# Folding a column Fourier transform a second time, in a fused attention and Fourier-mixing kernel

## Chip, cores and metric

The kernel runs on one core of one Trainium2 chip. The time is the device time of one execution in microseconds. A core has five engines that run their own instruction streams and wait for one another through semaphores: TensorE (PE, matmuls; PEld is its weight load), VectorE (DVE), ScalarE (ACT), GpSimd (POOL) and SyncE (SP, which here only starts DMAs).

## What is computed

Cosine attention over 8 batches, 12 heads, 448 tokens and 64 dimensions, then on its output (448 x 768 per batch) a two-dimensional Fourier transform of which the real part is kept, a residual, a layer norm and a two-layer feed-forward network. Cut to the core:

```python
q_n = q / (norm(q) + 1e-6); k_n = k / (norm(k) + 1e-6)
attn = softmax(q_n @ k_n.T / tau)
x = (attn @ v)                       # as (batch, 448, 768)
X = np.fft.fft(x, axis=1)            # over the sequence
X = np.fft.fft(X, axis=2)            # over the columns
u = x + np.real(X)
un = (u - mean(u)) / sqrt(var(u) + 1e-6)
out = u + np.maximum(un @ w_ch1, 0.0) @ w_ch2      # 768 -> 3072 -> 768
```

## The kernel before

The program first collects all its operations in a list (`P.add`: engine, function, estimated duration, priority, what is read and written), lays out an order for each engine with a small scheduler, and then emits the instructions in that order with the waits that the data need. An operation that two engines can do (`("act", "dve")`) goes to the one that the scheduler finds free first. Lower priority numbers are more urgent: batch b has 10 + 100 b and a little more, the evacuations of the feed-forward part have -1, its matmuls 5000 + b. So the attention of a batch goes ahead of the feed-forward matmuls of older batches, which fill the rest of TensorE's time.

The transform is done with real matrices. Rows and columns are folded first: with cosines only the sum of a row and its mirror image counts, with sines only their difference. `fold` is called for the column blocks dj = 0, 1, 2 of 128 columns, as soon as the two head pairs that it needs are done (`X[j]`, `X[j + 3]`). It takes sums and differences over the rows (AC), then of column c and c + 384 (F, one part for even and one for odd output columns), and multiplies each block with the sequence's cosines and sines:

```python
            if j >= 3:
                self.fold(b, j - 3, pj)
    ...
    def fold(self, b, dj, pj):
        ...
        for i, o in ((0, AluOp.add), (2, AluOp.subtract)):
            P.add("dve", ... v.tensor_tensor(AC[:, i:i + 2], X[:, 0:2], X[:, 2:4], o), ...)
        for eo, o in ((0, AluOp.add), (1, AluOp.subtract)):
            P.add("dve", ... v.tensor_tensor(F[:, eo, :, 128 * dj:128 * dj + 128],
                                             AC[:, :, 0, :], AC[:, :, 1, :], o), ...)
        def fn(pe):                                        # L828: 8 matmuls a block
            for eo in range(2):
                for s in range(2):
                    o = self.PS[:, bk + eo, s * NK:(s + 1) * NK]          # NK = 225
                    for t in range(2):
                        n = 128 if t == 0 else RB                         # RB = 97
                        r = pe.matmul(o, F[0:n, eo, 2 * s + t, dj * 128:dj * 128 + 128],
                                      self.CSs[0:n, t, s, :], start=(t == 0), stop=(t == 1))
        ...                                                # L839 (ACT) or L840 (DVE): PSUM to Tt
```

The column transform then takes all three blocks, for two tiles (kt) of sequence frequencies:

```python
        for kt in range(2):
            def fn(pe, tile=tile, kt=kt):                  # L863: 12 matmuls a tile
                for dj in range(3):
                    for s in (1, 0):
                        for eo in range(2):
                            m0, m1 = (0, 193) if eo == 0 else (193, 385)
                            o0 = (3 * eo + dj) * SQ2 + s * NK + 128 * kt
                            r = pe.matmul(PS[:, bk + s, m0:m1], self.Tt[:, o0:o0 + 128],
                                          self.CSd[:, dj, s, m0:m1], ...)
            ...           # L869, L872, L884: the two halves combined, x added, into U
```

The table CSd of cosines and sines for the columns (128 x 3 x 2 x 385) is made once, while batch 0's attention runs: its arguments by POOL and DVE (L403, L434, L439, L441, L442), the sines by ACT (L449, L450). After the transform comes the layer norm (L911 to L920; the normalised tile UN shares F's memory), then a transpose (for batch 0 by TensorE, later by DMA, L942), then the feed-forward part. Even batches have three tiles of 128 tokens, odd ones four, because one tile holds the last 64 tokens of two batches:

```python
        for ft in range(NF):                               # L974, L983/L984: relu(un @ w1)
            ...
        for i, ut in enumerate(tiles):                     # L995: hT @ w2
            for c in range(2):
                ...   # 24 matmuls of 384 columns, then on DVE (L1004) OUTB = PSUM + U
            if ut == A0:
                ...   # one plain store from SP
            else:
                ...   # one indirect store from POOL (L1019), rows in mirrored order
```

FFN b below means this part for batch b. While batch 0 is alone, idle time of TensorE is filled with matmuls whose result nobody reads (L1064).

The scheduler's rule for ACT and DVE, by which an engine that could start an operation at once may wait for a more urgent one instead (by at most 0.7 of the first one's duration):

```python
                    wait = tmin + 0.7 * op.durs[op.engs.index(e)]
                    t2, op2 = min((c for c in cands if c[0] <= wait), key=lambda c: (c[1].prio, c[0]))
                    if 109 <= op2.prio < 140 and op.prio > 200 or 9 <= op2.prio < 40 and (op.prio > 100 or op.prio > op2.prio + 0.5 and t2 < tmin + 0.25):
                        t, op = t2, op2
```

Of the kernel before, what the change touches and what calls it, by code (L numbers as in the profile page):

```python
# [12 lines left out]
DM = H * DH  # L13
# [8 lines left out]
ORDER = tuple(range(NJ))  # L22
# [39 lines left out]
class Plan:  # L62
# [54 lines left out]
    def schedule(self):  # L117
# [43 lines left out]
        while left:  # L161
            best = None
            for e in self.ENGS:
                cands = []
                for op in ready[e]:
                    rt = rtime(op, e)
                    if op.acquire is not None:
                        st = slot_time(op)
                        if st is None:
                            continue  # L170
                        rt = max(rt, st[0])
                    cands.append((max(rt, free[e]), op))
                if not cands:
                    continue
                tmin = min(c[0] for c in cands)
                t, op = min((c for c in cands if c[0] <= tmin + 1e-9), key=lambda c: (c[1].prio, c[1].seq))
                if e in ("act", "dve"):

                    wait = tmin + 0.7 * op.durs[op.engs.index(e)]
                    t2, op2 = min((c for c in cands if c[0] <= wait), key=lambda c: (c[1].prio, c[0]))  # L180
                    if 109 <= op2.prio < 140 and op.prio > 200 or 9 <= op2.prio < 40 and (op.prio > 100 or op.prio > op2.prio + 0.5 and t2 < tmin + 0.25):
                        t, op = t2, op2
                if best is None or (t, e) < best[:2]:
                    best = (t, e, op)
            t, e, op = best
            for e2 in op.engs:
                ready[e2].remove(op)
            op.eng = e
            if op.acquire is not None:
                for new, i in zip(op.acquire, slot_time(op)[1]):  # L190
                    old = slots[new.pool][i]
                    if old is not None:
                        op.deps.update(old.users)
                    slots[new.pool][i] = new
                    new.slot = i
            d = op.durs[op.engs.index(e)]
            op.start = t
            free[e] = t + d
            op.end = t + d
            if op.dma is not None:  # L200
                i = 1 if e == "pool" and op.name[:3] != "sc_" else 0
                t0 = max(op.end + DMA_LAT, dma_free[i])
                op.end = t0 + op.serve * (1.6 if dma_free[1 - i] > t0 else 1.0)
                dma_free[i] = op.end
            self.order[e].append(op)
            left -= 1
            for n in nxt.get(op, ()):
                cnt[n] -= 1
                if cnt[n] == 0:
                    put(n)  # L210
# [100 lines left out]
class Kern:  # L311

    def __init__(self, nc, q, k, v, w1, w2, out, tau, nb):
# [21 lines left out]
        self.X = T("X", [128, 4, DM])  # L335
        self.AC = T("AC", [128, 4, 2, 128])
        self.F = T("F", [128, 2, 4, DM // 2])
        self.Tt = T("Tt", [128, NJ * SQ2 + 32])
# [7 lines left out]
        self.CSd = T("CSd", [128, 3, 2, NL])  # L346
# [21 lines left out]
    def consts(self):  # L368
        P = self.P
        nd, ns = 3 * NL, 2 * NK  # L370
# [15 lines left out]
        def iotad(g):  # L386
            g.iota(self.rowf[:, 2:3], [[0, 1]], base=256, channel_multiplier=1, allow_small_or_imprecise_dtypes=True)
            g.iota(lcf[:, 0:193], [[2, 193]], base=0, channel_multiplier=0, allow_small_or_imprecise_dtypes=True)
            return g.iota(lcf[:, 193:385], [[2, 192]], base=1, channel_multiplier=0, allow_small_or_imprecise_dtypes=True)
# [7 lines left out]
        P.add("pool", iotad, 0.6, -7, "iotad", writes=["OUT1d", "rowg"])  # L397
# [24 lines left out]
        for p0, c0 in ((0, 64), (64, 129)):  # L422
# [3 lines left out]
                                 g.memset(self.Tt[:, NJ * SQ2:], 0.0))[-1],  # L426
# [4 lines left out]
        def args_d():  # L431
            P.add("pool", lambda g: prods(g, sd, lcf, 3, None, AluOp.mult), 3.75, 22, "tpd", reads=["OUT1d", "rowf", "rowg"],
                  writes=["tpd0", "tpd1", "tpd2"])
            P.add("pool", lambda g: g.tensor_scalar(Qt[:, sd], Pt[:, sd], 1.0 / DM, M, AluOp.mult, AluOp.add), 1.2, 23, "tqd",  # L434
                  reads=["tpd0", "tpd1", "tpd2"], writes=["tqd0", "tqd1", "tqd2"])
            for j in range(3):
                x, y = (a[:, NL * j:NL * j + NL] for a in (Pt, Qt))
                n = [f"tpd{j}", f"tqd{j}"]
                P.add("pool", lambda g, y=y: g.tensor_scalar(y, y, M, -float(DM), AluOp.subtract, AluOp.mult), 1.5, 25, "trd",  # L439
                      reads=n[1:], writes=n[1:])  # L440
                P.add("pool", lambda g, x=x, y=y: g.tensor_tensor(x, x, y, AluOp.add), 1.1, 25, "tad", reads=n, writes=n[:1])  # L441
                P.add("dve", lambda v, x=x, y=y: v.scalar_tensor_tensor(y, x, -1.0, x, AluOp.mult, AluOp.max), t_dve(NL), 30, "tmd",  # L442
                      reads=n, writes=n[1:])
        self.args_d = args_d

        def table(c, tab, n, k, sg, nm, pr, order, wr, t):
            def sins(a):
# [4 lines left out]
                         reads=[a + nm + x for a in ("tp", "tq") for x in ("012" if nm == "d" else [""])] + ["cst"], writes=[wr], order=order)  # L452
# [4 lines left out]
        self.table_d = lambda order: table(sd, self.CSd, DM, 3, -1, "d", 10, order, "CSd", 1.3)  # L457
# [227 lines left out]
    def attn(self, b):  # L685
# [34 lines left out]
        for pos, j in enumerate(ORDER):  # L720
# [78 lines left out]
            if j >= 3:  # L799
                self.fold(b, j - 3, pj)  # L800


    def fold(self, b, dj, pj):
# [3 lines left out]
        AC, F = self.AC, self.F  # L807
# [4 lines left out]
        for eo, o in ((0, AluOp.add), (1, AluOp.subtract)):  # L812
# [4 lines left out]
            if dj == 0 and eo == 0:  # L817
                self.first_f = op
        tile = Tile("G")

        def fn(pe):
            bk = self.bank(tile)
            for eo in range(2):
                for s in range(2):
                    o = self.PS[:, bk + eo, s * NK:(s + 1) * NK]
                    for t in range(2):
                        n = 128 if t == 0 else RB
                        r = pe.matmul(o, F[0:n, eo, 2 * s + t, dj * 128:dj * 128 + 128],  # L828
                                      self.CSs[0:n, t, s, :], start=(t == 0), stop=(t == 1))
            return r  # L830
        P.add("pe", fn, 8 * t_mm(NK), pj, f"fs{dj}_{b}", reads=[f"F0{dj}", f"F1{dj}", "CSs"], tiles=(tile,), acquire=tile, margin=0.2)

        for es, ah in ([(("act", "dve"), (0, 1))] if b == 0 and dj < 2 else [(("act",), (0,)), (("dve",), (1,))] if b == 0 else [(("act", "dve"), (0, 1))]):
            def ev(e, ah=ah):
                bk, a = self.bank(tile), slice(ah[0], ah[-1] + 1)
                o = self.Tt[:, 0:NJ * SQ2].rearrange("p (a d k) -> p d a k", a=2, d=3)[:, dj, a]
                i = self.PS[:, bk + ah[0]:bk + ah[-1] + 1, 0:SQ2]
                if e is self.nc.scalar:
                    return e.activation(o, i, ACTF.Copy)  # L839
                return e.tensor_copy(o, i)  # L840
            n = len(ah) * SQ2
            P.add(es, ev, [t_act(n) if e == "act" else t_dve(n) for e in es], pj, f"te{dj}_{b}",
                  writes=[f"Tt{dj}" + ("b" if len(ah) == 1 and ah[0] else "")], after=[tile.users[0]], tiles=(tile,))

    def fft(self, b):
# [6 lines left out]
        for kt in range(2):  # L852
            tile = Tile("G")

            def fn(pe, tile=tile, kt=kt):
                bk = self.bank(tile)

                for dj in range(3):
                    for s in (1, 0):
                        for eo in range(2):  # L860
                            m0, m1 = (0, 193) if eo == 0 else (193, 385)
                            o0 = (3 * eo + dj) * SQ2 + s * NK + 128 * kt
                            r = pe.matmul(PS[:, bk + s, m0:m1], self.Tt[:, o0:o0 + 128], self.CSd[:, dj, s, m0:m1],  # L863
                                          start=(dj == 0 and eo == 0), stop=(dj == 2 and eo == 1), skip_group_check=True)
                return r
            self.fd_ops.append(P.add("pe", fn, 12 * 0.081, pr + 1, f"fd{kt}_{b}", reads=["Tt0", "Tt1", "Tt2", "Tt2b", "CSd", "Tpad"],
# [36 lines left out]
        order = [A0, A1, Yt] if b % 2 == 0 else [A0, A1, Yt, Zt]  # L903
# [46 lines left out]


    def ffn(self, b):
# [3 lines left out]
        tiles = [A0, A1, Yt] if par == 0 else [A0, A1, Yt, Zt]  # L956
# [29 lines left out]
        for i, ut in enumerate(tiles):  # L986
            ob = self.out_next % 2
            self.out_next += 1
            for c in range(2):
                tile = Tile("M")  # L990
                for q4 in range(4):
                    def fn(pe, tile=tile, q4=q4, i=i, c=c):
                        bk = self.bank(tile)
                        for ft in range(6 * q4, 6 * q4 + 6):
                            r = pe.matmul(self.PS[:, bk, 0:384], self.hT[:, ft, 128 * i:128 * i + 128],  # L995
                                          self.W2b[:, ft, 384 * c:384 * c + 384], start=(ft == 0), stop=(ft == NF - 1))
                        return r
                    self.main = P.add("pe", fn, 6 * t_mm(384), PM, f"y{i}{c}{q4}_{b}",
# [3 lines left out]
                def fin(v, tile=tile, c=c, ut=ut, ob=ob):  # L1002
                    cs = slice(384 * c, 384 * c + 384)
                    return v.tensor_tensor(self.OUTB[:, ob, cs], self.PS[:, self.bank(tile), 0:384], self.U[:, ut, cs], AluOp.add)  # L1004
                rn = [f"U{ut}l", f"U{ut}h"] if ut != Zt else [f"U{ut}z{z}{x}" for z in (0, 64) for x in "lh"]
                P.add("dve", fin, t_dve(384), PEV, f"fin{i}{c}_{b}", reads=rn, writes=[f"OUT{ob}"] if c == 0 else [f"OUT{ob}b"],
                      after=(self.main,), tiles=(tile,))
            o = self.OUTB[:, ob, :]
# [114 lines left out]
```

## Time and profile before

| | |
|---|---|
| device time, median of 3 | 629.57 us (629.31 to 631.14) |
| span of the profiled execution | 629.2 us |
| busy: PE, DVE, ACT, POOL | 603.2, 382.8, 345.5, 97.7 us |
| sequence transform, L828 | 192 matmuls of 225 columns |
| column transform, L863 | 192 matmuls of 192 or 193 columns |
| feed-forward, L974 and L995 | 232.9 and 227.8 us busy |
| last matmul ends, span ends | 623.7, 629.2 us |

The page of a profile gives each engine's busy time, the same in 40 equal slices of the span, and the chain of work that ended last, followed back from the end; other views give the busy time in chosen stretches, the instructions in order of time, and who waited for whom. A line such as `L828 PE MATMUL PS<-CSs,F` names the line of the program, the engine, the operation, and what is written from what. Matmuls are pipelined, so the durations of single ones overlap.

### The profile page before, as it was taken

Reading aid. Unit: us, or ns where it says so; the run is one execution under the profiler, and the core shown is the slowest. Engines: PE = TensorE matmul, PEld = TensorE weight load, DVE = VectorE, ACT = ScalarE, POOL = GpSimd, SP = SyncE. Lnnn points to the kernel's source line nnn. Section 1 sums busy time; section 2 is a strip of 40 time slices with the busy share of each in tenths; the row PEclk is TensorE's granted clock in tenths of the full one; section 3 lists DMA queues with packets and bytes.
Section 4 is the critical chain, followed back from the end, with each engine's and each line's share of the span. In section 5 each row is a group of like instructions: output and inputs, shape, how many; then the busy total and the mean of one; then the engine's idle time right before and its main releaser. Section 6 shows DMA issues by size and latency. Waiting matters only on the chain.

```text
span 629.2 us, 13742 instructions
## 1 busy us (share of the span) xinstructions
PE 603.2 (96%) x5695; PEld 397.2 (63%) x5713; DVE 382.8 (61%) x869; ACT 345.5 (55%) x678; POOL 97.7 (16%) x129
## 2 busy tenths in 40 slices
PE   4798899999999999999999999999999999999996
PEld 4477677667876667665656765666566666654563
DVE  6978888896787876778777787747534550110011
ACT  7784797257862786376678638842864024114300
POOL 8822511110030102000300310003000010010001
PEclk8998999999999999999999999999999999999999
DMA  9999996977279517952973695139200130010011
GB/s 197 112 204 207 159 169 118 167 147 147 61 79 203 141 37 102 147 127 64 138 120 101 86 212 92 23 89 120 39 3 1 63 89 1 26 50 1 1 50 51
DMA packets 187486, 62.04 MB, mean 99 GB/s; under 512 B 166688, under 2 KB 185120, under 8 KB 187424
## 3 DMA queue, kind: packets, MB, share of 16 engines
q1 hardware_dynamic: 129504, 38.35, 32.9%
q0 software_dynamic: 57920, 22.81, 28.3%
q8 instruction: 45, 0.74, 0.5%
q14 instruction: 17, 0.14, 0.1%
HBM read 51.90 MB, written 11.01 MB: 100 GB/s over the span
## 4 chain that ended last, share of the span: by engine, by line
PE 91%; DVE 4%; ACT 3%; issue 1%; POOLq 0%; POOL 0%; ACTq 0%; DVEq 0%
PE PS L995 35%; PE PS L974 35%; PE PS L750 5%; PE PS L781 5%; PE PS L828 3%; PE PS L863 3%; PE PS L778 2%; ACT E L732 1%; PE PS L1064 1%; PE PS L610 1%; PE PS L762 1%; PE PS L763 1%; DVE UNT L574 1%; DVE UNT L570 0%; ACT E L544 0%
## 5 line engine op out<-in xcount | busy, mean ns | idle before, releaser
L974 PE MATMUL PS<-UNT,W1b 128*128 128x256 bf16 (+3 forms) x1422 | 232.9, 316 | 3.0 <-ACT hT L983 0.6
L995 PE MATMUL PS<-W2b,hT 128*128 128x384 bf16 x1344 | 227.8, 326 | 0.0
L974 PEld LDWEIGHTS PS<-UNT,W1b 128*128 128x128 bf16 x1440 | 129.9, 98 | 86.4 <-issue 4.9
L995 PEld LDWEIGHTS PS<-W2b,hT 128*128 128x128 bf16 x1344 | 129.4, 98 | 83.0 <-issue 1.8
L732 ACT ACTIVATE E<-PS 128x900 bf16<-128x900 f32 (+1 forms) x192 | 150.0, 826 | 29.3 <-PE PS L750 25.8
L983 ACT ACTIVATE hT<-PS 128x512 bf16<-128x512 f32 (+3 forms) x161 | 77.0, 478 | 100.7 <-PE PS L974 99.3
L1004 DVE TENSOR_TENSOR OUTB<-PS,U 128x384 f32<-128x384 f32 x56 | 31.1, 555 | 124.2 <-PE PS L995 123.7
L1019 POOL DMA_INDIRECT out_dram<-OUTB,IDX x20 | 21.3, 1064 | 307.7 <-DVE OUTB L1004 129.2
L984 DVE TENSOR_SCALAR hT<-PS 128x256 bf16<-128x256 f32 (+3 forms) x79 | 39.8, 505 | 25.8 <-PE PS L974 24.9
L667 DVE TENSOR_REDUCE SS<-QH 128x6 f32<-128x384 f32 x84 | 45.4, 541 | 11.2 <-ACT QH L665 11.0
L665 ACT ACTIVATE QH<-STG 128x384 f32<-128x384 f32 x84 | 43.6, 519 | 15.2 <-DVE SS L667 7.3
L781 PE MATMUL PS<-VB,E 128*128 128x65 bf16 x1152 | 51.3, 193 | 0.0
L712 POOL DMA_DIRECT2D VB<-in_v_dram x24 | 25.2, 1055 | 162.2 <-PE PS L781 161.6
L781 PEld LDWEIGHTS PS<-VB,E 128*128 128x128 bf16 x1152 | 47.8, 97 | 1.5
L750 PE MATMUL PS<-QT,KT 64*128 64x225 bf16 x576 | 43.0, 261 | 2.1 <-ACT E L732 1.6
L778 PE MATMUL PS<-VZ,E 128*128 128x130 bf16 x192 | 42.2, 220 | 0.0
L884 DVE TENSOR_TENSOR U<-SQT,X 128x384 bf16<-128x384 f32 (+3 forms) x80 | 41.0, 551 | 0.8
L674 DVE TENSOR_TENSOR QH<-STG,RN 128x768 bf16<-128x768 f32 x42 | 39.8, 952 | 1.3
L750 PEld LDWEIGHTS PS<-QT,KT 64*128 64x128 bf16 x576 | 21.2, 94 | 20.2 <-ACT E L732 7.2
L839 ACT ACTIVATE Tt<-PS 128x900 bf16<-128x900 f32 (+1 forms) x22 | 19.9, 904 | 25.6 <-PE PS L828 25.5
L795 DVE TENSOR_TENSOR X<-PS,RD 128x512 bf16<-128x512 f32 x48 | 33.1, 689 | 1.2
L793 DVE RECIPROCAL RD<-PS 128x8 f32<-128x8 f32 x48 | 9.8, 205 | 34.5 <-PE PS L781 34.4
(116 smaller groups left out, 498.8 us busy)
## 6 DMA issues: line engine op xcount, KB each, us to landing
STG<-in_q_dram SPq DMA_DIRECT2D x18, 384.0 KB, 6.0
STG<-in_k_dram SPq DMA_DIRECT2D x18, 384.0 KB, 4.6
VB<-in_v_dram POOLq DMA_DIRECT2D x24, 192.0 KB, 6.7
W1b<-in_moe_w_ch_dram POOLq DMA_DIRECT2D x12, 384.0 KB, 9.7
W2b<-in_moe_w_ch_dram POOLq DMA_DIRECT2D x12, 384.0 KB, 7.0
out_dram<-OUTB SPq DMA_DIRECT2D x8, 384.0 KB, 2.9
hT<-in_k_dram SPq DMA_DIRECT2D x2, 576.0 KB, 5.3
hT<-in_q_dram SPq DMA_DIRECT2D x2, 576.0 KB, 6.7
```

The source lines that it names most:

```text
L665: P.add("act", lambda a, sq=sq, src=buf[:, w * x:w * x + w]: a.activation(sq, src, ACTF.Square), t_act(w), pr, f"sq{i}_{b}", reads=bn, wri ...
L667: P.add("dve", lambda v, o=SS[:, i, H // ns * x:H // ns * (x + 1)], sq=sq: v.tensor_reduce(o, sq.rearrange("p (h d) -> p h d", d=DH), AX.X ...
L674: P.add("dve", lambda v, i=i, buf=buf, qh=qh: v.tensor_tensor(v3(qh), v3(buf), RN[:, i, :].unsqueeze(2).to_broadcast((128, H, DH)), AluOp. ...
L732: return a.activation(o, self.PS[:, bk:bk + nc_, 0:SQ2], ACTF.Exp, scale=1.0 / self.tau)
L750: i = pe.matmul(self.PS[:, bk + h, c0:c0 + NK], self.KT[r, jj, kt * 128:(kt + 1) * 128], self.QT[r, jj, cols], start=True, stop=True)
L778: pe.matmul(o, st(6), self.VZ[:, j, :], start=True, stop=False, skip_group_check=True)
L781: r = pe.matmul(o[:, 65 * h:65 * h + 65], st(2 * kt + h), self.VB[:, kt, 2 * j + h, :], start=False, stop=(h == 1 and kt == 2), skip_group ...
L884: return v.tensor_tensor(U[o0:o0 + n, ut, cs].rearrange("p (i e) -> p i e", e=2), src, X[i0:i0 + n, x, cs].rearrange("p (i e) -> p i e", e ...
L974: r = pe.matmul(self.PS[:, bk, 0:n], self.W1b[:, j, ft * 128:(ft + 1) * 128], unT[:, j, cs], start=(j == 0), stop=(j == NJ - 1))
L983: return e.activation(self.hT[:, ft, cs], self.PS[:, bk, 0:n], ACTF.Relu)
L984: return e.tensor_relu(self.hT[:, ft, cs], self.PS[:, bk, 0:n])
L995: r = pe.matmul(self.PS[:, bk, 0:384], self.hT[:, ft, 128 * i:128 * i + 128], self.W2b[:, ft, 384 * c:384 * c + 384], start=(ft == 0), sto ...
```

## The change

A second fold is put on top of the first. Column c of F and column 384 - c (with sum and difference, for cosine and sine) go into one column of a new array G of 193 columns, so that the transforms have a block of 128 and one of 65 columns in place of three of 128. Block 0 can be made after dj = 0 and dj = 2, block 1 after dj = 1, so the head pairs are taken in the order 0, 1, 2, 3, 5, 4. The two columns without a partner (0 and 192) are copied by POOL. The table CSd and its making shrink from three blocks to two; POOL clears all of Tt once. ACT and DVE may now wait for a more urgent operation of any older batch, not of batches 0 and 1 alone. And the last batch takes the tiles in another order, so that the very last store is a plain one from SP, done in two parts of 512 and 256 columns. The diff, cut:

```diff
-ORDER = tuple(range(NJ))
+NG = DM // 4 + 1
+ORDER = (0, 1, 2, 3, 5, 4)
@@ schedule
-                    if 109 <= op2.prio < 140 and op.prio > 200 or 9 <= op2.prio < 40 and (op.prio > 100 or op.prio > op2.prio + 0.5 and t2 < tmin + 0.25):
+                    if op2.prio >= 9 and (op.prio > op2.prio + 60 or op2.prio < 40 and op.prio > op2.prio + 0.5 and t2 < tmin + 0.25):
@@ buffers and tables
+        self.G = T("G", [128, 2, 4, NG])
-        self.Tt = T("Tt", [128, NJ * SQ2 + 32])
+        self.Tt = T("Tt", [128, 4 * SQ2 + 32])
-        self.CSd = T("CSd", [128, 3, 2, NL])
+        self.CSd = T("CSd", [128, 2, 2, NL])
-                                 g.memset(self.Tt[:, NJ * SQ2:], 0.0))[-1],
+                                 g.memset(self.Tt[:], 0.0))[-1],
-            for j in range(3):        # arguments of CSd, a block each
+            for j in range(2):
@@ fold
-            if j >= 3:
+            if pos >= 3:
                 self.fold(b, j - 3, pj)
+        if dj < 2:
+            c = 192 * dj
+            P.add("pool", lambda g: g.tensor_copy(G[:, :, :, c:c + 1], F[:, :, :, c:c + 1]), 0.25, pj, f"gc{dj}_{b}", ...)
+        if dj == 0:
+            return
+        blk = 2 - dj if dj == 2 else 1
+        c0, n, m = ((1, 127, 128), (128, 64, 65))[blk]
+        for i, o in ((0, AluOp.add), (1, AluOp.subtract)):
+            def fn(v, i=i, o=o):
+                ...
+                return v.tensor_tensor(gp(G[:], [[gs, 2], [NG, 2], [1, n]], g0 + c0), gp(F[:], [[fs_, 2], [384, 2], [1, n]], f0 + c0),
+                                       gp(F[:], [[fs_, 2], [384, 2], [-1, n]], f0 + 384 - c0), o)
+            P.add("dve", fn, t_dve(4 * n), pj, f"g{blk}_{b}", ...)
-                        r = pe.matmul(o, F[0:n, eo, 2 * s + t, dj * 128:dj * 128 + 128],
-                                      self.CSs[0:n, t, s, :], start=(t == 0), stop=(t == 1))
+                        r = pe.matmul(o, G[0:k, eo, 2 * s + t, blk * 128:blk * 128 + m],
+                                      self.CSs[0:k, t, s, :], start=(t == 0), stop=(t == 1))
@@ fft
-                for dj in range(3):
+                for d in range(2):
+                    k = 128 if d == 0 else NG - 128
...
-                            r = pe.matmul(PS[:, bk + s, m0:m1], self.Tt[:, o0:o0 + 128], self.CSd[:, dj, s, m0:m1],
+                            r = pe.matmul(PS[:, bk + s, m0:m1], self.Tt[0:k, o0:o0 + 128], self.CSd[0:k, d, s, m0:m1],
@@ feed-forward
+        return [A0, A1, Yt, Zt] if b < self.nb - 1 else [A1, Yt, Zt, A0]
...
+            very_last = b == self.nb - 1 and i == len(tiles) - 1
+            for c, (c0, c1) in enumerate(((0, 512), (512, 768)) if very_last else ((0, 384), (384, 768))):
...
+                if very_last:
+                    P.add("sp", ... sy.dma_start(<out, rows of the tile, columns c0:c0 + n>, self.OUTB[:, ob, c0:c0 + n]) ...)
```

## The prediction
> **What bounds the kernel now.** I read the page first (busy shares, then the slices), then the windows table of the whole span, then the chain that ended last, then the timelines of the stages in which the chain leaves TensorE.
>
> The page's first two parts:
>
> ```profile
> PE 603.2 (96%) x5695; PEld 397.2 (63%) x5713; DVE 382.8 (61%) x869; ACT 345.5 (55%) x678; POOL 97.7 (16%) x129
> ...
> PE   4798899999999999999999999999999999999996
> ...
> DVE  6978888896787876778777787747534550110011
> ...
> PEclk8998999999999999999999999999999999999999
> ```
>
> From the sixth slice on TensorE (PE) is never under nine tenths. The windows table, cut where the stages change (columns: stretch, its length, PE, weight loads, DVE, ACT, POOL busy, then clock and DMA):
>
> ```profile
> 0.00:56.40 56.40, 40.44 (x763) 33.02 (x764) 43.42 (x91) 40.98 (x60) 34.12 (x56) 0.92 1.13 181
> 56.40:134.20 77.80, 74.75 (x812) 55.16 (x810) 67.39 (x162) 49.69 (x114) 18.82 (x25) 0.99 1.07 154
> 134.20:485.30 351.10, 349.83 (x3322) 230.58 (x3338) 246.16 (x566) 226.26 (x448) 36.84 (x41) 1.00 0.65 99
> 485.30:623.70 138.40, 138.23 (x802) 78.45 (x802) 25.23 (x52) 28.60 (x57) 7.01 (x7) 1.00 0.10 35
> 623.70:629.20 5.50, 0.00 (x0) 0.00 (x0) 0.56 (x1) 0.00 (x0) 0.96 (x1) 0.90 0.18 72
> ```
>
> So there are four regimes. To 56.4 us a prologue, batch 0 alone, in which PE also runs filler matmuls and the path goes through DVE and ACT. To 134 us a stretch in which DVE is busy 67.4 of 77.8 us (87%) and PE 96%. From 134 to 623.7 us PE is idle for 1.27 + 0.17 = 1.4 us in all, so there a matmul taken away is time taken away. Last a tail of 5.5 us without PE. Because a busy PE need not be PE at its peak, I took the cost of the transform not from busy time but from the chain, which lists back-to-back steps (start, length, what). Batch 2:
>
> ```profile
> 178.07 0.79 PE PS L828 x8
> ...
> 181.01 0.79 PE PS L828 x8
> ...
> 189.58 0.79 PE PS L828 x8
> 190.37 1.95 PE PS L995 x12
> 192.32 2.02 PE PS L863 x24
> ```
>
> L828 is the sequence transform of one block (8 matmuls of 225 columns), L863 the column transform (24 matmuls of 192 or 193). Each sits directly in PE's chain, with the second feed-forward product (L995) around it.
>
> [...]the chain has 0.79/8 = 99 ns and 2.02/24 = 84 ns[...]. [...]the new 65-column weights should not be dearer than today's 128 columns (98 ns shown, hidden behind matmuls). No run here shows 65 yet. [...]
>
> **The change, part by part.**
>
> *Steady state, batches 2 to 7.* Sequence transform: three blocks become two, minus 1 x 0.79 us. Column transform: 24 matmuls become 2 tiles x 2 blocks x 2 x 2 = 16, minus 8 x 84 ns = 0.67 us. Together 1.46 us of PE time per batch, all on PE's path; six batches give 8.8 us. Added on DVE are four folding adds a batch, two of 508 and two of 256 elements. At the rate of the present pairs (two of 512 in 0.76 us) that is 0.76 + 0.5 = about 1.3 us a batch[...]. Taken from ACT: one eviction of 128x900, 0.92 us. Added on POOL: two copies of 8 elements, like the 6-element copies of L704 (212 to 805 ns). In this stretch DVE is 70% busy and ACT 64%, and the attention of a batch runs ahead of its feed-forward part (the last column transform is at 483 us, its feed-forward part starts at 561). So I count nothing for the additions.
>
> *Batch 1, 56 to 134 us.* Same PE saving, but FFN 1 has to have its input. The normalised second tile and the transposes on the way to it, and FFN 1's first matmul:
>
> ```profile
> 127.51 5.76 SPq L942 DMA_TRANSPOSE UNT<-F  x4
> 128.40 0.46 DVE L920 TENSOR_SCALAR F<-U,MV,RS 128x768 bf16<-128x768 bf16 x1
> 132.45 1.65 PE L974 MATMUL PS<-UNT,W1b 128*128 128x256 bf16 x12
> ```
>
> FFN 1 begins with two tiles. The second is normalised at 128.86 and its transpose lands a median 2.5 us after issue, about 131.5 us by my estimate. Spare time: 0.95 us. PE would arrive 1.46 us earlier, so at least 0.5 us of the saving becomes a wait; the DVE adds lengthen the wait and the eviction taken from ACT (91% busy from 80 to 100 us, 18.53 of 20) shortens it. I keep 0.7 of the 1.46 us.
>
> *Prologue, batch 0.* Its PE savings only make room for fillers. What counts is the other engines. Timeline of 26 to 33 us, and below it from the chain:
>
> ```profile
> 29.02 1.62 DVE L574 TENSOR_TENSOR UNT<-hT,RN 128x384 bf16<-128x384 f32 x1
> 29.20 1.02 POOL L441 TENSOR_TENSOR U<-U,UNT 128x385 f32<-128x385 f32 x1
> ...
> 31.24 0.54 DVE L442 SCALAR_TENSOR_TENSOR UNT<-U 128x385 f32<-128x385 f32 x1
> ```
>
> ```profile
> 39.65 0.93 ACT Tt L839
> ```
>
> The first lasts 1.62 us where its neighbours last 0.55: POOL's third table step runs beside it. With a table of two blocks the third POOL step is gone (minus 1.07 us on DVE), and so is the third L442 (minus 0.54). The eviction at 39.65 stands between exponentials on ACT and is gone for that position (minus 0.93). Back come the folding adds: the larger pair fits mostly into the gap of 1.1 us that DVE has before L840 at 42.5 us; the smaller pair is on the end of the chain (plus 0.5 to 0.75), and the first tile of the column transform ends 4 x 84 = 0.34 us sooner. Sum: -1.07 - 0.54 - 0.93 + 0.7 - 0.34 = -2.2 us. Now POOL also clears the whole of Tt at the start, 1,832 columns; by VZ's clearing (780 columns, 0.87 us) an estimate of 2 us, against 1.25 us saved in the first table step (3.74/3). I keep 1.7 of 2.2 us.
>
> *Tail.*
>
> ```profile
> 623.79 0.56 DVE L1004 TENSOR_TENSOR OUTB<-PS,U 128x384 f32<-128x384 f32 x1 [3.36 <-PE PS L995]
> ...
> 625.16 0.96 POOL L1019 DMA_INDIRECT out_dram<-OUTB,IDX  x1 [6.95 <-DVE OUTB L1004]
> ```
>
> Today a 384-column addition, then 0.8 us until POOL starts, then 3.1 us until an indirect store lands, then 0.9 us to the end. Afterwards: 256 columns ([...]0.43 us) and a plain store from SP. SP's full-tile stores land in 2.9 us; for a third of the bytes I estimate 2.4. 0.1 + 0.43 + 0.05 + 2.4 + 0.9 = 3.9 us against 5.5: minus 1.6 us. The products of the last tile cost PE the same in sum (24 x 512 + 24 x 256 columns, as 48 x 384).
>
> *The waiting rule and the order of heads.* They decide who goes first on DVE and ACT; for batches 0 and 1 the old rule did nearly the same already, and later PE does not wait for either. I count 0. Sum: -8.8 - 0.7 - 1.7 - 1.6 = -12.8 us, so 629.6 - 12.8 = 616.8 us.
>
> **The rivals.** (a) *DVE becomes the bound in 56 to 134 us.* For it: 87% busy, and only 0.95 us to spare before FFN 1. Against it: 10.4 us of DVE idle in that stretch. If all four adds of batches 0 and 1 (up to 4 us) delayed FFN 1, the gain of the prologue and of batch 1 would be gone: about 620 us. (b) *A wait for POOL takes the place of the matmuls.* The sequence transform now waits for a POOL copy, in a queue that holds loads of V (three of 1.05 us right after the last product of a batch) and stores. If each of 14 copies held PE for 0.3 us: 4 us, 620.5 us. Against it: these loads start some 3 us before the copy is due (246.72 to 249.86, the last fold done at 249.56), and the program's order was laid out with more than their real length. (c) *Only the count of matmuls moves*, the prologue being bound elsewhere: -8.8 - 0.7 - 1.6, 618.5 us. (d) *Everything lands*: batch 1 and the prologue in full, 1.3 us more: 615 us or a little under.
>
> **Range and chances.** 616.8 us as the middle; (a) and (b) in part give the upper end, 620.5, and (d) with a warmer prologue clock (0.92 on average now) the lower, 613.5. A 2% gain needs 617.0 us, which is almost my middle: 0.52 for faster, 0.47 for within 2%. Slower by 2% would need a stall of over 25 us, where PE has next to none: 0.01.
>
> **What would show each step right or wrong.** L828's successor with 128 matmuls, 0.79 us per block of 8, and the column transform with 128 in 1.35 us per batch; PE idle from FFN 1's start to the end of PE under 2 us; FFN 1's start about 3 us earlier with a short wait for the transposed input; the first feed-forward matmul near 54.7 us; a tail under 4 us. It is wrong if PE's list of waits names POOL copies or G, if FFN 1's first matmul waits for more than 2 us, if blocks of 65 weight columns take longer than 0.79 us, or if the first feed-forward matmul comes no earlier than 56.4 us.

## The result, and the profile after

The changed kernel takes 626.16 us (median of 4, 625.57 to 627.76), the kernel before beside it 630.36 us; the ratio is 0.9938, 95% interval 0.9911 to 0.9965. So it is faster by 0.6%, where 2.0% was predicted, and outside the predicted range.

The page's busy shares and slices of the changed kernel show at once where to look:

```profile
PE 594.1 (95%) x5607; PEld 388.3 (62%) x5625; DVE 391.3 (63%) x893; ACT 342.7 (55%) x677; POOL 98.4 (16%) x141
...
PE   4784889999999999999999999999999999999998
...
PEclk9996899999999999999999999999999999999999
```

PE has 9.1 us less busy time than before, but its fourth slice (47 to 63 us) has fallen to four tenths, and the clock that it was granted there to six. The windows table, with the same cuts as before:

```profile
0.00:56.40 56.40, 33.53 (x624) 27.20 (x625) 37.64 (x80) 35.73 (x52) 31.85 (x54) 0.90 1.13 182
56.40:134.20 77.80, 73.61 (x911) 57.14 (x910) 63.39 (x147) 48.13 (x104) 17.71 (x24) 0.96 0.91 122
134.20:485.30 351.10, 349.32 (x3278) 225.63 (x3291) 263.93 (x615) 229.85 (x464) 40.81 (x55) 1.00 0.66 105
```

In the prologue all four engines have less work done at 56.4 us than before; DVE 37.6 us in place of 43.4. None of them has become the bound; all of them wait. From 134 us PE is as full as before. PE's list of waits (what waited for what, us in all, times, longest) names the one long wait that is new:

```profile
PE PS L847 <- POOL G L823: 9.4, 1, 9.4
PE PS L1097 <- DVE ID L430: 5.6, 1, 5.6
PE PS L599 <- DVE QH L575: 1.8, 1, 1.8
```

L847 is the sequence transform, L823 the POOL copy of the columns without a partner. It is one single wait of 9.4 us. POOL's own timeline of 39 to 56 us tells why the copy came late:

```profile
39.90 0.82 POOL L470 DMA_DIRECT2D W1b<-in_moe_w_ch_dram  x1 [2.73 <-DMA W1b<-in_moe_w_ch_dram]
40.76 0.51 POOL L823 COPY G<-F 128x8 bf16<-128x8 bf16 x1
45.58 0.84 POOL L470 DMA_DIRECT2D W1b<-in_moe_w_ch_dram  x1 [4.31 <-DMA W1b<-in_moe_w_ch_dram]
48.84 0.82 POOL L470 DMA_DIRECT2D W1b<-in_moe_w_ch_dram  x1 [2.42 <-DMA W1b<-in_moe_w_ch_dram]
54.07 0.82 POOL L470 DMA_DIRECT2D W1b<-in_moe_w_ch_dram  x1 [4.41 <-DMA W1b<-in_moe_w_ch_dram]
54.89 0.23 POOL L823 COPY G<-F 128x8 bf16<-128x8 bf16 x1
```

POOL issues the loads of W1, and each load waits (in brackets: idle time, and what ended it) for the load three before it to have landed. The program's order has batch 0's second copy behind the last three of these issues. The data were ready at about 45 us. DVE's last fold, which the copy reads, ends at 44.96, and the last folding add, which the transform also needs, at 45.5:

```profile
44.20 0.76 DVE L814 TENSOR_TENSOR F<-AC 128x512 bf16<-128x512 bf16 x2
45.00 0.51 DVE L834 TENSOR_TENSOR G<-F 128x256 bf16<-128x256 bf16 x2
```

The copy itself takes 0.23 us; it stood in the queue for 10 us. The chain that ended last now goes through transfers there, which it did nowhere before:

```profile
23.58 8.36 DMA W1b<-in_moe_w_ch_dram
...
32.23 7.39 DMA W1b<-in_moe_w_ch_dram
...
39.90 13.89 DMA W1b<-in_moe_w_ch_dram
...
54.07 0.82 POOL W1b L470
...
55.17 1.72 PE PS L847 x8
```

The rest of the chain shows what was meant to come. Batch 2's two sequence blocks and its column transform:

```profile
196.04 0.79 PE PS L847 x8
...
199.75 0.79 PE PS L847 x8
...
202.50 1.36 PE PS L882 x16
```

There are two blocks of 0.79 us where there were three, and 1.36 us where there were 2.02. The tail, shown by the last two instructions but the end of the DMA:

```profile
621.46 2.61 SPq L1036 DMA_DIRECT2D out_dram<-OUTB  x2
623.29 0.42 DVE L1031 TENSOR_TENSOR OUTB<-PS,U 128x256 f32<-128x256 f32 x1 [1.90 <-PE PS L1022]
```

With four marks in each trace the whole difference can be entered in a small account. The first matmuls of FFN 0 in the two kernels, and of FFN 1 in the changed one, are these (that of FFN 1 before was at 132.45 us):

```profile
56.41 8.81 PE L974 MATMUL PS<-UNT,W1b 128*128 128x128 bf16 x108
```

```profile
65.76 2.50 PE L1000 MATMUL PS<-UNT,W1b 128*128 128x128 bf16 x22 [0.17 <-ACT UNT L958]
...
140.19 0.82 PE L1000 MATMUL PS<-UNT,W1b 128*128 128x256 bf16 x6
```

The account in us; the third column is the first experiment below:

| | before | after | copies on DVE |
|---|---|---|---|
| start to first matmul of FFN 0 | 56.41 | 65.76 | 54.69 |
| from there to the first of FFN 1 | 76.04 | 74.43 | 74.07 |
| from there to the end of PE | 491.2 | 483.0 | 483.0 |
| tail | 5.5 | 2.7 | 2.7 |
| span | 629.2 | 625.9 | 614.5 |

The change gained 1.6, 8.2 and 2.8 us in the last three stages, and lost 9.35 us in the first. Each column is one execution, and executions of one kernel differ by 2 to 4 us: the traced one was the slowest of four for the changed kernel (627.76 us) and the fastest of four for the experiment (616.30), so their spans lie 11.4 us apart, the medians 8.8.

### The profile page after: what moved, and what is told of

Same layout as the page of the kernel before. It is cut to its first block, busy times and chain, and to the rows that moved or that the text cites. A ratio compares the mean times of both kernels' runs of the same rounds, so it can differ in the third digit from the quotient of the medians.

```text
span 625.9 us, 13629 instructions
## 1 busy us (share of the span) xinstructions
PE 594.1 (95%) x5607; PEld 388.3 (62%) x5625; DVE 391.3 (63%) x893; ACT 342.7 (55%) x677; POOL 98.4 (16%) x141
## 4 chain that ended last, share of the span: by engine, by line
PE 85%; DMA 5%; POOL 4%; DVE 3%; ACT 2%; issue 1%; POOLq 0%; DVEq 0%
PE PS L1000 35%; PE PS L1022 33%; PE PS L751 5%; PE PS L782 5%; DMA W1b<-in_moe_w_ch_dram 5%; PE PS L847 2%; PE PS L779 2%; PE PS L882 2%; ACT E L733 1%; DVE U L903 1%; PE PS L763 1%; PE PS L764 1%; POOL VB L713 1%; POOL UNT L440 0%; DVE ST L930 0%
## 5 line engine op out<-in xcount | busy, mean ns | idle before, releaser
L1022 PE MATMUL PS<-W2b,hT 128*128 128x384 bf16 (+2 forms) x1343 | 228.9, 326 | 0.1
L733 ACT ACTIVATE E<-PS 128x900 bf16<-128x900 f32 (+1 forms) x192 | 149.8, 826 | 32.1 <-PE PS L751 26.6
L1009 ACT ACTIVATE hT<-PS 128x512 bf16<-128x512 f32 (+3 forms) x166 | 79.6, 480 | 99.5 <-PE PS L1000 98.0
L1031 DVE TENSOR_TENSOR OUTB<-PS,U 128x384 f32<-128x384 f32 (+2 forms) x56 | 31.2, 557 | 117.6 <-PE PS L1022 116.8
L668 DVE TENSOR_REDUCE SS<-QH 128x6 f32<-128x384 f32 x84 | 45.3, 540 | 11.5 <-ACT QH L666 11.3
L1010 DVE TENSOR_SCALAR hT<-PS 128x256 bf16<-128x256 f32 (+3 forms) x74 | 37.0, 501 | 23.1 <-PE PS L1000 21.8
L857 ACT ACTIVATE Tt<-PS 128x900 bf16<-128x900 f32 (+2 forms) x14 | 12.5, 892 | 40.5 <-PE PS L847 40.5
L934 ACT ACTIVATE RS<-MV,cst 128x1 f32<-128x1 f32 x28 | 8.2, 291 | 42.4 <-DVE MV L932 41.1
```

The lines of the kernel that those rows point to most:

```text
L668: P.add("dve", lambda v, o=SS[:, i, H // ns * x:H // ns * (x + 1)], sq=sq: v.tensor_reduce(o, sq.rearrange("p (h d) -> p h d", d=DH), AX.X ...
L733: return a.activation(o, self.PS[:, bk:bk + nc_, 0:SQ2], ACTF.Exp, scale=1.0 / self.tau)
L1009: return e.activation(self.hT[:, ft, cs], self.PS[:, bk, 0:n], ACTF.Relu)
L1010: return e.tensor_relu(self.hT[:, ft, cs], self.PS[:, bk, 0:n])
L1022: r = pe.matmul(self.PS[:, bk, 0:n], self.hT[:, ft, 128 * i:128 * i + 128], self.W2b[:, ft, c0:c0 + n], start=(ft == 0), stop=(ft == NF - 1))
```

## Experiments

In the text below "the mended kernel" is the changed kernel with batch 0's copies on DVE.

**Batch 0's copies on DVE.**

```diff
-            P.add("pool", lambda g: g.tensor_copy(G[...], F[...]), 0.25, pj, f"gc{dj}_{b}", ...)
+            P.add("dve" if b == 0 else "pool", lambda g: g.tensor_copy(G[...], F[...]), 0.25, pj, f"gc{dj}_{b}", ...)
```

> Batch 0's two copies of columns 0 and 192 are made by DVE in place of POOL; the orders of all engines are otherwise those of the changed kernel. Theory (place in POOL's queue): the second copy no longer stands behind three weight loads that wait for earlier loads, so the last sequence transform of batch 0 starts near 45.8 us in place of 55.2, FFN 0 near 56, and the time falls by 9 to 10 us, to 616 to 617.5 us. Rival 1 (weights): W1 lands no sooner, so FFN 0, started sooner, waits for W1 instead, and the time stays above 622 us. Rival 2 (DVE): the folding adds hold back batches 0 and 1, so that FFN 1 starts no sooner than 137 us and the time stays above 620 us.

617.33 us (ratio to the kernel before 0.9821, 0.9796 to 0.9846). Its PE timeline, the second sequence block of batch 0 and the first matmuls of FFN 0 and FFN 1:

```profile
45.21 0.96 PE L847 MATMUL PS<-CSs,G 128*65 128x225 bf16 x8
...
54.69 8.68 PE L1000 MATMUL PS<-UNT,W1b 128*128 128x128 bf16 x108
...
128.76 0.82 PE L1000 MATMUL PS<-UNT,W1b 128*128 128x256 bf16 x6
```

The block starts 10 us sooner, and FFN 0 and FFN 1 each 11 us sooner than in the changed kernel. In the two traces all engines have the same order of instructions (TensorE's fillers left aside), except that the two copies have gone from POOL to DVE. FFN 0 doesn't wait for its weights, and FFN 1 starts well ahead of 137 us: both rivals fall.

**The copies stay on POOL, the loads go behind them.** So that it is the place and not the engine that changes:

```diff
-            prev.append(P.add("pool", fn, 0.8, 9, nm, ..., after=[prev[-3]], serve=2.1))
+            prev.append(P.add("pool", fn, 0.8, 9, nm, ..., after=[prev[-3]] + ([self.gc] if i >= 9 else []), serve=2.1))
...
-            P.add("pool", lambda g: g.tensor_copy(G[...], F[...]), 0.25, pj, f"gc{dj}_{b}", ...)
+            self.gc = P.add("pool", lambda g: g.tensor_copy(G[...], F[...]), 0.25, pj, f"gc{dj}_{b}", ...)
```

> The copies stay on POOL; the last three W1 loads are put behind the second copy of batch 0. Theory (place in POOL's queue): as without POOL, 616 to 617.5 us, last sequence transform of batch 0 near 45.9 us. Rival (POOL itself is slow at the copy, or slowed by DVE): the transform starts later than 47 us and the time stays above 618.5 us. Rival (weights): the three loads, now issued a little later, hold FFN 0: above 620 us.

617.53 us (0.9815, 0.9797 to 0.9834). One copy has moved up in POOL's order; the orders of the other engines are those of the changed kernel (fillers left aside). POOL's timeline:

```profile
44.68 0.35 POOL L823 COPY G<-F 128x8 bf16<-128x8 bf16 x1 [4.48 <-DVE F L814]
45.57 0.84 POOL L470 DMA_DIRECT2D W1b<-in_moe_w_ch_dram  x1 [0.54 <-POOL G L823]
```

The copy now waits for DVE's fold and for nothing else, and the load behind it is issued at 45.57 us, just when it was issued before (45.58). POOL is fast enough at the copy; its queue was the cause.

**The same queue, without any second fold.** In the kernel before, one more POOL copy, of 8 elements a partition, that batch 0's last sequence transform waits for:

```diff
+        gd = []
+        if b == 0 and dj == 2:
+            P.add("pool", lambda g: g.tensor_copy(self.GD[:], F[:, :, :, 320:321]), 0.25, pj, "gd",
+                  reads=[f"F0{dj}", f"F1{dj}"], writes=["GD"])
+            gd = ["GD"]
...
-        P.add("pe", fn, 8 * t_mm(NK), pj, f"fs{dj}_{b}", reads=[f"F0{dj}", f"F1{dj}", "CSs"], ...)
+        P.add("pe", fn, 8 * t_mm(NK), pj, f"fs{dj}_{b}", reads=[f"F0{dj}", f"F1{dj}", "CSs"] + gd, ...)
```

> The kernel before, three blocks, with one more POOL copy of 8 columns in batch 0 which its last sequence transform waits for. Theory (place in POOL's queue): the copy lands behind the last W1 loads here too, the transform starts near 55 us in place of 46.1, and the time grows by 8 to 10 us to 638 to 640 us. Rival (the delay came from the second fold: its adds, its narrower block, its later order): the time stays within 1.5 us of 630.

640.36 us (1.017, 1.0147 to 1.0193). The first line of PE's waits (L834 is the sequence transform here):

```profile
PE PS L834 <- POOL GD L822: 8.8, 1, 8.8
```

A copy of 0.2 us costs 10.9 us with three blocks, where it cost 8.8 with two (medians). So the wait does not need the second fold.

**Tail as before**, on the mended kernel:

```diff
-        return [A0, A1, Yt, Zt] if b < self.nb - 1 else [A1, Yt, Zt, A0]
+        return [A0, A1, Yt, Zt]
...
-            very_last = b == self.nb - 1 and i == len(tiles) - 1
+            very_last = False
```

> As the run with batch 0's copies on DVE, but with the old order of tiles and the old stores in the last batch. From the trace of the changed kernel (tail of 2.7 us after the last matmul, 5.5 us before): 2.8 us more than with the new tail, 619 to 620 us. If the tail is worth only what the prediction said, 1.6 us more.

619.18 us (0.9831, 0.9813 to 0.9849), 1.85 us more than the mended kernel; the two intervals overlap, so the times alone don't fix the size. The trace does better: its last matmul ends at 611.97 us, the mended kernel's at 611.77, and the spans end at 617.2 and 614.5. That is 5.2 us of tail against 2.7.

**The old waiting rule**, on the mended kernel:

```diff
-                    if op2.prio >= 9 and (op.prio > op2.prio + 60 or op2.prio < 40 and op.prio > op2.prio + 0.5 and t2 < tmin + 0.25):
+                    if 109 <= op2.prio < 140 and op.prio > 200 or 9 <= op2.prio < 40 and (op.prio > 100 or op.prio > op2.prio + 0.5 and t2 < tmin + 0.25):
```

> As the run with batch 0's copies on DVE (617.3 us), but with the old waiting rule of ACT and DVE. The prediction counted 0 for the rule, since TensorE does not wait for either engine after the prologue: 617.3 us, within 1 us. Rival (the rule is part of the gain, because it brings older batches through sooner): more than 1.5 us slower, 619 us or more, with idle time of TensorE after 134 us above 3 us.

624.99 us (0.993, 0.9907 to 0.9952), 7.7 us slower than the mended kernel. My expectation was wrong and the rival right. The windows table of the kernel with the old rule:

```profile
128.80:195.00 66.20, 65.93 (x677) 48.37 (x675) 50.62 (x125) 43.74 (x99) 7.79 (x11) 1.00 0.69 117
195.00:225.00 30.00, 22.96 (x244) 15.04 (x242) 20.88 (x48) 17.07 (x36) 2.12 (x3) 1.00 0.95 144
225.00:480.00 255.00, 254.72 (x2329) 158.09 (x2330) 187.06 (x434) 162.66 (x317) 31.86 (x41) 1.00 0.64 94
```

and the middle stretch of the mended kernel:

```profile
195.00:225.00 30.00, 30.00 (x281) 18.68 (x279) 22.53 (x53) 18.97 (x39) 1.96 (x2) 1.00 0.56 120
```

Nearly all of the loss, 7.04 us of idle PE, lies between 195 and 225 us. The column transform of batch 2 comes at 197.2 us in place of 190.9. FFN 1's last matmuls end at 210.9 us and FFN 2's first starts at 220.3; in the mended kernel it is 209.4 and 211.2. What put batch 2 back is most likely work on the norms of the next batch: between 150 and 175 us DVE makes 12 of their sums (L668) in place of 8, and ACT 17 of the exponentials (L733) in place of 19. That this is the whole of it was not tested.

**The new rule alone**, on the kernel before (the diff above, the other way round):

> The kernel before with the new waiting rule of ACT and DVE alone; three blocks, nothing else changed. With the second fold in place, the old rule cost 7.7 us (the kernel without the second fold's queue wait: 617.3 us with the new rule, 625.0 with the old), all of it TensorE idle between 195 and 225 us, when FFN 1 had run out before batch 2 was ready. Theory (the rule is only worth something once TensorE has less to do, because the kernel before has no such idle time): 629.6 us, within 1.5 us. Rival (the rule is a gain of its own): 625 us or less.

630.04 us (1.0008, 0.9995 to 1.0022). Alone the rule does nothing that shows. The four combinations:

| | old rule | new rule |
|---|---|---|
| three blocks (the kernel before) | 629.64 | 630.04 |
| two blocks, mended | 624.99 | 617.33 |

**Each folding add made twice**, on the mended kernel:

```diff
+            P.add("dve", fn, t_dve(4 * n), pj, f"h{blk}_{b}", reads=..., writes=[f"G{blk}{i}"])
```

> As the run with batch 0's copies on DVE (617.3 us), with each of the four folding adds of a batch made a second time, with the same result: about 1.3 us more on DVE per batch, on the way to the sequence transforms too. Theory (the adds cost time only where DVE is on the path, in batches 0 and 1): 0.5 to 2.5 us more, 618 to 620 us. Rival (DVE has become the bound): at least 1.3 us for each of six batches more, 625 us or above.

622.22 us (0.988, 0.9851 to 0.9908), 4.9 us more than the mended kernel: above what the theory allowed and below the rival. Between the two traced executions it is 5.5 us. FFN 0 starts at 56.03 us (1.3 later), FFN 1 at 132.56 (3.8 later). So about seven tenths are lost before FFN 1, and the other six batches cost 1.7 us. In batch 0 PE now waits for the adds themselves (L849 is the sequence transform here):

```profile
PE PS L849 <- DVE G L834: 2.4, 1, 2.4
```

What PE waited for from 132 us to the end:

```profile
PE PS L1002 <- DMA UNT<-F: 1.6, 1, 1.6
PE PS L751 <- ACT E L733: 1.2, 2, 0.9
PE PS L1002 <- ACT hT L1011: 0.7, 1, 0.7
```

The first is the wait for FFN 1's transposed input. Not all of the 4.9 us need be DVE's work, since the scheduler moved other operations too: TensorE's fillers end at 39.5 us here (200 of them) and at 54.4 in the mended kernel (448), and the clock that PE was granted up to the start of FFN 0 was 0.85 on average (0 to 56.0 us) in place of 0.93 (0 to 54.7 us).

**All copies on DVE:**

```diff
-            P.add("pool", lambda g: g.tensor_copy(...
+            P.add("dve", lambda g: g.tensor_copy(...
```

> All 16 copies of columns 0 and 192 on DVE, not batch 0's alone. If POOL copies cost nothing where feed-forward matmuls fill TensorE: as with batch 0's alone, 617.3 us, within 1 us. Rival (each POOL copy holds TensorE a little): 1.5 to 4 us faster, 613 to 616 us.

618.11 us (0.9807, 0.9779 to 0.9835), the same as the mended kernel within the uncertainty. The POOL copies of batches 1 to 7 cost nothing that shows there. The traced execution was one of 619.59 us; its FFN 0 starts at 57.95 us, 3.3 later than in the mended kernel's trace, though up to there the orders of the engines are the same. The stages behind it differ by about half a microsecond.

**A truer load time for the scheduler:**

```diff
-... after=[prev[-3]], serve=2.1))
+... after=[prev[-3]], serve=4.0))
```

> The changed kernel with one number altered: the scheduler is told that a weight load takes 4.0 us of transfer in place of 2.1. The copy stays on POOL, but the program's order then has it before the last four W1 loads of the nine that come last, not behind them all. Theory (the order came out of a load time that was estimated too low): last sequence transform of batch 0 at 45 to 46.5 us, and 616 to 619 us. Rival (the place of the copy does not matter by itself): 624 us or more. The orders of the other engines change with it in later batches, which may add or take a microsecond.

638.22 us (1.012, 1.0087 to 1.0152). The first half of the expectation came true: the copy is placed ahead of the last four W1 loads, the transform starts at 45.93 us and FFN 0 at 56.30. The total did not: the whole layout changed with the number, and FFN 1 starts only at 152.49 us. In POOL's timeline a load of W2 now stands behind a copy of batch 1:

```profile
110.81 0.21 POOL L823 COPY G<-F 128x8 bf16<-128x8 bf16 x1 [18.62 <-DVE F L814]
111.57 0.72 POOL L471 DMA_DIRECT2D W2b<-in_moe_w_ch_dram  x1 [0.54 <-POOL G L823]
```

In the mended kernel the last load of W2 is issued at 95.8 us. Batch 1's last sequence transform, too, now waits 2.3 us for a POOL copy. How much of the loss is due to this late load, and how much to other moves in the layout, was not separated. So the run shows that the order follows from the estimated load time, but not that a better estimate gives a better kernel.

## Why the prediction was wrong

**The step that failed** is the prologue, "I keep 1.7 of 2.2 us" as a gain, together with what spoke against rival (b): "these loads start some 3 us before the copy is due". That was read from the V loads of a later batch. For batch 0 I listed the engines' work, but not what POOL's queue holds when the copy falls due, although the timeline of the kernel before shows POOL at 42 to 54 us with W1 issues that each wait 2.5 to 4.6 us for a transfer:

```profile
42.74 0.82 POOL L469 DMA_DIRECT2D W1b<-in_moe_w_ch_dram  x1 [4.56 <-DMA W1b<-in_moe_w_ch_dram]
46.89 0.82 POOL L469 DMA_DIRECT2D W1b<-in_moe_w_ch_dram  x1 [3.33 <-DMA W1b<-in_moe_w_ch_dram]
50.24 0.82 POOL L469 DMA_DIRECT2D W1b<-in_moe_w_ch_dram  x1 [2.53 <-DMA W1b<-in_moe_w_ch_dram]
54.19 0.82 POOL L469 DMA_DIRECT2D W1b<-in_moe_w_ch_dram  x1 [3.12 <-DMA W1b<-in_moe_w_ch_dram]
```

A copy put into that queue inherits those waits. The other reason against (b), that the order was laid out with more than the loads' real length, does not hold for W1: the scheduler reckons with 2.1 us of transfer a load (3.4 beside other transfers), and in the changed kernel three loads in a row went out 4.7 us apart on average (39.90 to 54.07 us). The term should have been 9.35 us of loss in place of 1.7 of gain: 11 us off, against 9.4 us between the predicted and the measured time. Two of the prediction's own signs of being wrong came: PE's list of waits names G, and the first feed-forward matmul came later than 56.4 us. While PE waited, the clock that it was granted fell too, to a mean of 0.55 from 50 to 60 us, where the kernel before has 0.83; the block behind the wait took 1.72 us in place of 0.96:

```profile
50.00:60.00 10.00, 7.90 (x162) 7.29 (x157) 8.79 (x20) 4.20 (x11) 2.34 (x3) 0.83 1.30 212
```

```profile
50.00:60.00 10.00, 4.83 (x57) 4.66 (x58) 0.93 (x2) 1.04 (x2) 1.75 (x3) 0.55 1.34 212
```

**Without the queue wait the prologue was right in its direction.** In the mended kernel's trace FFN 0 starts 1.7 us before the old time, where 1.7 was kept. That the figures agree is luck: with the same order of engines up to there, the traces of the tail and of the all-copies experiment have 55.05 and 57.95 us. The POOL step beside which L574 took 1.62 us is gone, and the same operation takes 0.55 us now; the larger pair of folding adds takes 0.77 us and the smaller 0.51, where the pairs of 512 forward elements take 0.76, so the reversed operand costs nothing that shows; clearing Tt takes 1.62 us where 2 were estimated.

**Batch 1:** 0.7 us kept of 1.46; from FFN 0's start to FFN 1's the mended kernel gains 2.0 us, the changed one 1.6. Of the wait of 0.5 us or more that was expected at FFN 1, 0.4 us shows, and it is for an addition on DVE, not for the transposed input; where the gain above 1.46 comes from stays open. (ACT's 18.53 of 20 us, in the prediction's argument here, are 93%, not 91.) Rival (a), DVE as the bound there, did not come about with four adds. With eight, this stage is 2.5 us longer than in the mended kernel.

**Steady state:** minus 8.8 us predicted, minus 8.2 measured, with 0.79 us per block and 1.36 us for the column transform, as worked out. The cost was right, but not what the gain depends on:

**The waiting rule:** "I count 0" gave no error in the sum, but by luck, since the reason was wrong ("later PE does not wait for either"). That was read from the kernel before, and holds there: the rule alone changes nothing that shows. In the kernel with two blocks the feed-forward matmuls that had covered batch 2's preparation run out, and under the old rule 7.7 of the second fold's microseconds come back as idle time. In this layout the rule is what lets the fold have its effect. Whether PE's smaller share of work does it, DVE's four added operations, or the order that the scheduler happened to lay out, was not separated; one altered number cost 12 us in the run with 4.0.

**Tail:** minus 1.6 predicted, minus 2.8 measured. The 256-column addition took 0.42 us where 0.43 was estimated. The mis-sized term is the time from the last addition to the end, 0.05 + 2.4 + 0.9 = 3.35 us estimated; from the addition's end at 623.71 to the end of the span at 625.9 it is 2.2 us.

The prediction's sum, which had no queue wait, was 616.8 us, and the mended kernel takes 617.33. The closeness is partly luck: measured on the two traces the four terms are -1.7, -2.0, -8.2 and -2.8, together 14.7 us in place of 12.8, and the trace is of the fastest execution.

## What to carry to other kernels

A small operation given to an idle engine is not free if that engine's queue also issues transfers that wait for other transfers (here a copy of 0.23 us held PE for 9.4 us): ask what stands ahead of it in program order when it falls due, above all while weights are loaded, and put it on another queue or ahead of those issues. And work taken off the bounding engine uses up the slack that hid other chains: what made no difference before (here the rule on who goes first) can be worth more than half of the gain afterwards, so test such parts in both settings.

## What the runs showed of the hardware

In the changed kernel, from 60 us on, weight loads of 65 columns took 111 to 112 ns each on average, those of 128 columns 98 to 99 ns, so the smaller block has the dearer load. (Over the whole span the 65-column mean is 119 ns, with batch 0's loads at the fallen clock among them: 0.55 from 50 to 60 us.) It stays hidden behind matmuls of 225 columns: 0.79 us per block of 8 either way. That the smaller load would not be dearer was the author's expectation, and these figures go against it.

Matmuls overlap: one of 225 columns is listed with 260 ns, and 8 of them, with their loads, take 0.79 us, 99 ns each. For the 192 or 193 columns of the column transform it is 85 ns (1.36 us for 16). Half of the matmuls in a sequence block have 97 rows in place of 128, and are listed with the same 261 ns.

A bfloat16 addition on DVE with one operand read backwards took as long as a forward one: 426 ns for 508 elements, against 421 for 512 forward (means of the changed kernel).
